# Snake activation by a cosine identity over pairs of PSUM banks, alpha folded into the weights, one stock of banks, a planned order

## The chip, the cores and the metric

The kernel runs on one core of a Trainium2 chip. The time is device microseconds (us) of one launch, as the median of several runs. A core has five engines that run in order, each on its own queue, and meet by semaphores: PE (TensorE), DVE (VectorE), ACT (ScalarE), POOL (GpSimd) and SP, which here only issues DMAs.

## The reference

```python
f = 1 / (1 + exp(-f_logit))                      # q, k, v, f_logit: (4, 8, 768, 48)
for t in range(768):
    state = f[t][:, None] * state + outer(k[t], v[t])
    y[t] = q[t] @ state
x = y, heads side by side                        # (3072, 384)
h = x @ w_in                                     # (3072, 2048)
s = sin(alpha * h)                               # alpha: one number per column of h
out = (h + s * s / (alpha + 1e-9)) @ w_out       # (3072, 384)
```

## The kernel before

The 768 steps are cut into 6 chunks c of 128 steps. A chunk has four batches b, handled in halves: a unit u = 2c + half is two batches. For each unit SP loads f, k, q and v (128x768 float32, 384 KB each, 48 loads in rows of 192 bytes) into three buffers of each kind (`load`).

**Attention.** `pre` (L316 on): ACT turns f into log decay (L327, L330), PE sums it over time with a triangular mask (cs, L350), ACT makes the decay and its inverse (G in place in PSUM, L359; Gi, L363), and two products scale k and q (L372). `attend`: PE transposes them (tp), a copy brings them to SBUF (tr, L416; from chunk 4 on a DMA transpose does both), PE makes scores in two banks (aps, L425), DVE masks each bank by itself (at, L428), PE adds the old state's part and the scores' part (y), and y is copied and transposed into xT (from chunk 3 on by DMA). The state is renewed by kv, sum and st.

**MLP.** `first`: for each of 16 blocks fb of 128 columns, PE makes h (three matmuls of 128x512, one bank; L542), ACT takes the sine with alpha as its scale (L547), somebody squares it (L555 on POOL or DVE, L553 on ACT), and DVE adds (square / alpha) + h into the bfloat16 g (L560). Chunk 0 does this by halves of 256 tokens. `second`: for each batch, 16 matmuls of 128x384 over the blocks g (o, L580), a copy (osb) and a store.

**Banks and order.** PSUM's eight banks are split: 2 for o, 3 for h, 3 for all else. The weights are cast to bfloat16 by DMAs on POOL's queue, held back until certain loads have landed (`weights_after`). The order on each engine comes from a planner, `in_order`, which starts the operation that could begin first by its own table of durations, with tables of biases (KIND, ON_ACT, ...) fitted to it.

Of the kernel before, what the change touches and what calls it, by code (L numbers as in the profile page):

```python
# [71 lines left out]

class Op:
    after, line, on_act = 0, None, 0

    def __init__(self, rank, engs, emit, deps, takes, table, dma):
        self.rank, self.engs, self.emit, self.deps, self.takes = rank, engs, emit, deps, takes
        self.table, self.dma, self.start, self.end, self.eng = table, dma, None, None, None
        self.line = table and "table"


LATENCY = {"PE": 260, "ACT": 160, "DVE": 180, "POOL": 180, "SP": 0}
TABLE_LOAD, DMA_LATENCY, DMA_AHEAD = 1280, 1400, 1000


def in_order(ops, lines):


    free = dict.fromkeys(("PE", "ACT", "DVE", "POOL", "SP"), 2500)
    free["ACT"] = free["SP"] = 800  # L90
    dma_free, table = dict.fromkeys(("SP", "POOL"), 0), None
    follows = {}
    for o in ops:
        for d in set(o.deps):
            follows.setdefault(d, []).append(o)
    missing = {o: len(set(o.deps)) for o in ops}
    done, turn, nth = [], {o: i for x in lines.values() for i, o in enumerate(x)}, dict.fromkeys(lines, 0)

    def when(o):

        t = max([o.after] + [d.end + (LATENCY[d.eng] if d.eng not in o.engs or len(o.engs) > 1 or d.eng != "PE" else 0)
                             for d in o.deps])
        for j, b in enumerate(o.takes):
            if b.place is None:
                i = len(b.ring.taken) + sum(x.ring is b.ring for x in o.takes[:j])
                if i >= b.ring.n:
                    old = b.ring.taken[i - b.ring.n]
                    if any(x.end is None for x in old.users):
                        return None
                    t = max([t] + [x.end + LATENCY[x.eng] for x in old.users])  # L110
        return t

    pending = [o for o in ops if not missing[o]]
    left = len(ops)
    while left:
        best = None
        for o in pending:
            if o.line and turn[o] != nth[o.line]:
                continue
            t = when(o)  # L120
            if t is None:
                continue
            for e, dur in o.engs.items():
                s = max(t, free[e])
                if o.dma:
                    s = max(s, dma_free[e] - DMA_AHEAD)
                d = dur + (TABLE_LOAD if o.table and o.table != table and table else 0)
                key = (s + (BIAS[e] + (o.on_act if e == "ACT" else 0) if len(o.engs) > 1 else 0), o.rank, s + d)
                if best is None or key < best[0]:
                    best = (key, o, e, s, d)  # L130
        if best is None:
            raise RuntimeError("no operation can start")
        _, o, e, s, d = best
        o.start, o.eng, free[e] = s, e, s + d
        o.end = s + d
        if o.dma:
            dma_free[e] = max(s + 600, dma_free[e]) + o.dma
            o.end = dma_free[e] + DMA_LATENCY + (1500 if e == "POOL" else 0)
            if e == "POOL":
                dma_free["SP"] = max(s + 600, dma_free["SP"]) + o.dma  # L140
        table = o.table or table
        if o.line:
            nth[o.line] += 1
        for b in o.takes:
            if b.place is None:
                b.place = len(b.ring.taken)
                b.ring.taken.append(b)
        pending.remove(o)
        for x in follows.get(o, ()):
            missing[x] -= 1  # L150
            if not missing[x]:
                pending.append(x)
        done.append((o, e))
        left -= 1
    return done
# [518 lines left out]
```

## Time and profile before

| | |
|---|---|
| three runs | 217.67, 219.94, 220.72 us, median 219.94 |
| span of the profiled execution | 216.7 us, first to last instruction; that execution's own time is not among the numbers given, and the three runs lie 1.0 to 4.0 us above its span |
| PE, DVE, ACT, POOL busy | 182.6, 157.3, 165.9, 102.4 us |
| mean share of the DMA engines | 72.0% by SP's queue, 9.1% by POOL's |

A busy PE is not a PE at its full rate, since the matmul rows hold their latency too. So the rate is read where matmuls stand back to back, and the work left is counted in matmuls.

### The profile page before, as it was taken

To read this page: it belongs to the slowest core of one execution; us is meant where nothing else is said; L and a number is where in the kernel's file an instruction comes from. 1 tells how busy PE (TensorE), PEld (TensorE's weight loads), DVE (VectorE), ACT (ScalarE), POOL (GpSimd) and SP (SyncE) were. 2 spreads that over 40 slices of the span, in tenths; PEclk is the share of its full clock that TensorE was granted. 3 is DMA by queue.
4 is the path that set the end of the run, shared out by engine and by line. 5 is a ranking of instruction groups with operands and counts; after the bars stand their busy time and mean duration, and the time that the engine had idled before them with its cause. 6 is when DMAs were issued, how large, how long until landed. Compare 5 with 4: busy or idle time off the path is not lost.

```text
span 216.7 us, 4268 instructions
## 1 busy us (share of the span) xinstructions
PE 182.6 (84%) x1537; PEld 107.5 (50%) x1537; DVE 157.3 (73%) x290; ACT 165.9 (77%) x272; POOL 102.4 (47%) x131
## 2 busy tenths in 40 slices
PE   0477785489968999858899987989999999999993
PEld 0345553257655645534565533555554555555551
DVE  2364895475794799897779989579989968787800
ACT  3578778966579979878998999886778888667711
POOL 5334692863543488677575412685324113233100
PEclk9999999658999999979999999999999999999999
DMA  7999999999999999799799993834701211010211
GB/s 130 187 187 217 197 200 187 199 187 199 181 192 190 181 191 168 184 148 155 173 188 182 188 183 93 190 60 146 168 20 39 94 54 41 0 73 2 74 73 73
DMA packets 119733, 30.30 MB, mean 140 GB/s; under 512 B 113040, under 2 KB 119712, under 8 KB 119712
## 3 DMA queue, kind: packets, MB, share of 16 engines
q1 hardware_dynamic: 115968, 26.88, 72.0%
q0 software_dynamic: 3744, 3.15, 9.1%
q8 instruction: 12, 0.20, 0.4%
q14 instruction: 9, 0.07, 0.2%
HBM read 25.17 MB, written 4.72 MB: 138 GB/s over the span
## 4 chain that ended last, share of the span: by engine, by line
PE 59%; DVE 16%; DMA 9%; ACT 5%; issue 5%; SPq 3%; POOL 2%; ACTq 0%; POOLq 0%; DVEq 0%
PE o L580 25%; PE h L542 23%; DMA f<-in_f_logit_dram 6%; DVE g L560 6%; DVE at L428 4%; DMA v<-in_v_dram 3%; SPq L270 3%; PE tp L408 3%; PE aps L425 2%; DVE vb L334 2%; PE y L445 2%; POOL s L555 2%; PE cs L350 1%; DVE sum L481 1%; ACT f L327 1%
## 5 line engine op out<-in xcount | busy, mean ns | idle before, releaser
L555 POOL TENSOR_TENSOR s<-s 128x512 f32<-128x512 f32 (+1 forms) x71 | 61.0, 872 | 64.0 <-ACT s L547 56.5
L547 ACT ACTIVATE s<-h,al_p 128x512 f32<-128x512 f32 (+1 forms) x112 | 67.5, 627 | 22.4 <-PE h L542 18.7
L542 PE MATMUL h<-xT,w_in_bf 128*128 128x512 bf16 (+1 forms) x336 | 78.3, 355 | 6.8 <-DVE g L560 4.8
L580 PE MATMUL o<-w_out_bf,g 128*128 128x384 bf16 x384 | 79.1, 332 | 2.5 <-DVE g L560 2.3
L560 DVE SCALAR_TENSOR_TENSOR g<-s,al_r,h 128x512 bf16<-128x512 f32 (+1 forms) x112 | 72.3, 666 | 10.3 <-POOL s L555 7.4
L580 PEld LDWEIGHTS <-g 128*128 128x128 bf16 x384 | 35.8, 99 | 27.8 <-DVE g L560 3.6
L542 PEld LDWEIGHTS <-w_in_bf 128*128 128x128 bf16 x336 | 32.3, 99 | 31.7 <-issue 8.7
L428 DVE TENSOR_TENSOR at<-aps,mask 128x512 bf16<-128x512 f32 x48 | 31.7, 684 | 4.7 <-PE aps L425 4.5
L372 POOL TENSOR_TENSOR qk<-k,Gi 128x384 bf16<-128x384 f32 x22 | 21.9, 1007 | 24.2 <-ACT Gi L363 24.1
L372 DVE TENSOR_TENSOR qk<-q,cs 128x384 bf16<-128x384 f32 x24 | 13.2, 549 | 11.0 <-ACT cs L359 10.4
L553 ACT ACTIVATE s<-s 128x512 f32<-128x512 f32 x28 | 17.6, 633 | 0.7
L350 PE MATMUL cs<-lf,mask 128*128 128x384 bf16 x24 | 8.2, 358 | 11.0 <-ACT lf L330 9.7
L416 ACT COPY tr<-tp 128x1024 bf16<-128x1024 bf16 x12 | 12.1, 1014 | 3.1 <-PE tp L408 3.0
L642 ACT ACT_TABLE_LOAD x11 | 14.1, 1283 | 0.2
L408 PE MATMUL tp<-ident,qk 128*128 128x128 bf16 x128 | 12.2, 255 | 2.4 <-POOL qk L372 1.9
L363 ACT ACTIVATE Gi<-cs 128x384 f32<-128x384 f32 x24 | 11.6, 485 | 2.6 <-PE cs L353 1.3
L425 PE MATMUL aps<-tr 64*128 64x128 bf16 x192 | 10.9, 231 | 3.1 <-ACT tr L416 2.1
L327 ACT ACTIVATE f<-f 128x768 f32<-128x768 f32 x12 | 10.1, 839 | 4.2 <-DMA f<-in_f_logit_dram 2.8
L485 POOL TENSOR_TENSOR st<-sum,gl 128x384 bf16<-128x384 f32 x12 | 10.2, 860 | 5.7 <-DVE sum L481 5.7
L445 PE MATMUL y<-vb,at 128*128 128x48 bf16 x192 | 11.5, 190 | 1.3 <-DVE at L428 0.7
L408 PEld LDWEIGHTS <-qk 128*128 128x128 bf16 x128 | 10.4, 117 | 4.3 <-POOL qk L372 2.6
L359 ACT ACTIVATE cs<-cs 128x388 f32<-128x388 f32 (+1 forms) x24 | 11.5, 480 | 0.6
(53 smaller groups left out, 150.8 us busy)
## 6 DMA issues: line engine op xcount, KB each, us to landing
f<-in_f_logit_dram SPq DMA_DIRECT2D x12, 384.0 KB, 6.7
k<-in_k_dram SPq DMA_DIRECT2D x12, 384.0 KB, 6.7
q<-in_q_dram SPq DMA_DIRECT2D x12, 384.0 KB, 6.8
v<-in_v_dram SPq DMA_DIRECT2D x12, 384.0 KB, 6.7
out_dram<-osb SPq DMA_DIRECT2D x24, 192.0 KB, 1.9
w_in_bf<-in_moe_w_in_dram POOLq DMA_DIRECT2D x4, 384.0 KB, 8.1
w_out_bf<-in_moe_w_out_dram POOLq DMA_DIRECT2D x4, 384.0 KB, 7.8
xT<-yn SPq DMA_TRANSPOSE x12, 2.3
```

The costliest lines, as they stand in the source:

```text
L372: engine[e].tensor_mul(qk_b[bufs["qk", m].place % NQ][:, "kq".index(n), :, :, :D], tl[n, u][:, i * H:(i + 1) * H, :].rearrange("c (r p) d ...
L408: nc.tensor.transpose(tl[x, "tp"][:, j * HP + p, :], qk_b[qkb.place % NQ][:, j, p, :, :].rearrange("c r e -> c (r e)"), ident)
L425: nc.tensor.matmul(aps[r][:, p, :], t[halves[r], p, :], t[halves[r], HP + p, :], start=True, stop=True)
L428: nc.vector.tensor_mul(tl[x, "at", r], tl[x, "a"][r], mask4)
L445: nc.tensor.matmul(tl[x, "y"][:, h * D:(h + 1) * D], tl[x, "at", r][:, p, :], v_b[vb.place % NV][:, i, h, :], start=(first and p == r == 0 ...
L542: nc.tensor.matmul(h[:, :n], w_in_bf[:, kb, fs], xT[:, ts.start // C:ts.stop // C, kb, :], start=(kb == 0), stop=(kb == KB - 1))
L547: nc.scalar.activation(out=s[:, :n], in_=tl[x, "h"][:, :n], func=Act.Sin, scale=al_p[:, fb:fb + 1])
L553: nc.scalar.activation(out=s2[:, :n], in_=s[:, :n], func=Act.Square)
L555: engine[e].tensor_mul(s2[:, :n], s[:, :n], s[:, :n])
L560: nc.vector.scalar_tensor_tensor(tl["g", c, fb][:, ts], tl[x, "s2"][:, :n], al_r[:, fb:fb + 1], tl[x, "h"][:, :n], Alu.mult, Alu.add)
L580: nc.tensor.matmul(tl["o", c, t], tl["g", c, fb][:, t * P:(t + 1) * P], w_out_bf[:, fb, :], start=(fb == 0), stop=(fb == FB - 1))
L642: nc.scalar.preload_act_table_set(now)
```

## The change

- **Identity.** sin² a = (1 - cos 2a) / 2. `w_in` is multiplied by -2 alpha and `w_out` by -1 / (2 (alpha + 1e-9)). PE then gives h' = -2 alpha h, ACT takes sin(h' + pi/2), and one DVE instruction makes g' = (s - 1) + h'. The 112 squares are gone.
- **Weights.** They come as float32 on SP's queue into three staging buffers `wst` and are folded by eight multiplications (six on POOL, two on DVE). The factor for `w_in` is alpha spread over 128 partitions by four float32 matmuls of one row.
- **Two banks at once.** In chunks 1 to 5 h is made in pairs of blocks in two banks, and sine and addition run once over 128x1024. The masks do the same for the scores. In chunk 0 a pair of half blocks shares one bank.
- **One stock of banks.** All eight banks are one tile, and each buffer's bank comes from the order table.
- **G in SBUF.** The decay leaves PSUM, so POOL can take q's products: it has 17 of them (DVE 7), 18 of k's (DVE 6), and 10 of the 12 casts of v (none before). Of the tr copies DVE makes 14 (4 before), ACT 2 (12 before).
- **Order.** The planner is replaced by a list of 982 numbers (operation, engine, bank), found beforehand.

```diff
+ORDER = [10, 74, 75, 83, 10077, 22, 20008, 85, 2088, 9, 84, 78, 14, 30004, 11, 2005, 137, 138, 40000, 50006,
...
+SLOTS = dict(f=3, k=3, q=3, v=3, lf=2, qk=6, vb=4, gl=6, Gi=4, tr=4, at=3, xT=2, yn=5, s=3, g=18, G=3, osb=3, sum=2,
+             wst=3, st0=2, st1=2, st2=2, st3=2)
...
-    ps_o = pool("ps_o", 2, space=bass.MemoryType.PSUM)
-    ps_h = pool("ps_h", N_H, space=bass.MemoryType.PSUM)
-    ps_a = pool("ps_a", N_A, space=bass.MemoryType.PSUM)
+    banks = psum.tile([P, 8, 512], F32, name="banks")
...
+    nc.vector.memset(ones_f, -2.0)
...
+                nc.tensor.matmul(ps(b, 512), ones_f, al_row[:, fs], start=True, stop=True)
...
+            nc.vector.tensor_scalar(al_r, ps(b, FB), 1e-9, -2.0, Alu.add, Alu.mult)
             nc.vector.reciprocal(al_r, al_r)
...
-                nc.gpsimd.dma_start(out=w_in_bf[:, :, fs], in_=moe_w_in[:, fs].rearrange("(kb p) f -> p kb f", p=P))
...
+        def ld(e):
+            engine[e].dma_start(out=view(), in_=src)
+
+        def fold(e):
+            engine[e].tensor_tensor(dst, view(), fac(), Alu.mult)
+        l = op({SP: 500}, ld, takes=[b], dma=2050)
...
-            g = tl["cs", m][:, :n_G]
-            nc.scalar.activation(out=g, in_=g, func=Act.Exp, scale=-1.0)
...
+                nc.scalar.activation(out=at(Gb)[:, :n_G], in_=ps(cb, n_G), func=Act.Exp, scale=-1.0)
...
-            nc.vector.tensor_mul(tl[x, "at", r], tl[x, "a"][r], mask4)
...
+            nc.vector.tensor_mul(at(atb), ps(ab, 1024).rearrange("c (r p t) -> c r p t", r=2, p=HP),
+                                 mask4.unsqueeze(1).to_broadcast([C, 2, HP, C]))
...
+            nc.scalar.activation(out=at(sb)[:, :n], in_=ps(hb, n), func=Act.Sin, bias=quarter)
...
+            nc.vector.scalar_tensor_tensor(take(at(gb)), at(sb)[:, :n].rearrange("p (j t) -> p j t", j=2), -1.0,
+                                           ps(hb, n).rearrange("p (j t) -> p j t", j=2), Alu.add, Alu.add)
...
-            nc.scalar.activation(out=s[:, :n], in_=tl[x, "h"][:, :n], func=Act.Sin, scale=al_p[:, fb:fb + 1])
...
-                nc.scalar.activation(out=s2[:, :n], in_=s[:, :n], func=Act.Square)
...
-                engine[e].tensor_mul(s2[:, :n], s[:, :n], s[:, :n])
...
-            nc.vector.scalar_tensor_tensor(tl["g", c, fb][:, ts], tl[x, "s2"][:, :n], al_r[:, fb:fb + 1],
-                                           tl[x, "h"][:, :n], Alu.mult, Alu.add)
```

The first place is the weights. Before, POOL issues their DMAs itself, early (`seen` is the wait for a load; the last two rows are a product for k and the first square):

```order
L372 TENSOR_TENSOR qk_87<-k_133,Gi_153 128x8x48
L372 TENSOR_TENSOR qk_88<-k_133,Gi_156 128x8x48
L285 COPY seen<-f_160 1x1
L292 DMA w_in_bf<-in_moe_w_in_dram 128x3x512
L285 COPY seen<-q_183 1x1
L292 DMA w_in_bf<-in_moe_w_in_dram 128x3x512 x3
L372 TENSOR_TENSOR qk_90<-k_218,Gi_299 128x8x48
L555 TENSOR_TENSOR s_0_0_0_370<-s_0_0_314 128x256
```

In the change they stand on SP's queue between the loads. These are its DMAs number 11 to 22, counted from the first load of f:

```order
L219 DMA k_70<-in_k_dram 128x16x48
L219 DMA q_73<-in_q_dram 128x16x48
L219 DMA f_67<-in_f_logit_dram 128x16x48
L274 DMA wst_142<-in_moe_w_in_dram 128x3x512
L274 DMA wst_143<-in_moe_w_in_dram 128x3x512
L274 DMA wst_144<-in_moe_w_in_dram 128x3x512
L219 DMA v_76<-in_v_dram 128x16x48
L274 DMA wst_142<-in_moe_w_in_dram 128x3x512
L274 DMA wst_143<-in_moe_w_out_dram 128x4x384
L274 DMA wst_144<-in_moe_w_out_dram 128x4x384
L219 DMA q_71<-in_q_dram 128x16x48
L219 DMA k_68<-in_k_dram 128x16x48
```

So the first weights moved behind 13 loads, and the first part of `w_out` is DMA number 19; the last part of `w_in` (number 18) and all of `w_out` reuse a staging buffer and wait for its fold.

The second place is DVE in the middle of the program, chunk 2, where blocks of the MLP and masks of the attention alternate. Before:

```order
L555 TENSOR_TENSOR s_1_10_0_1560<-s_10_0_1527 128x512
L560 SCALAR_TENSOR_TENSOR g_10_1578<-s_1_10_0_1560,al_r,h_10_0_1421 128x512
L428 TENSOR_TENSOR at_0_0_1564<-aps_0_0_1566,mask_97 128x512
L428 TENSOR_TENSOR at_0_1_1565<-aps_0_1_1567,mask_97 128x512
L560 SCALAR_TENSOR_TENSOR g_11_1607<-s_1_11_0_1589,al_r,h_11_0_1461 128x512
```

And now, in chunks 2 and 3:

```order
L461 SCALAR_TENSOR_TENSOR g_126<-s_115,banks 128x1024
L409 TENSOR_TENSOR sum_141<-banks,st_145 128x384
L412 TENSOR_TENSOR st_152<-sum_140,gl_91 128x384
L409 TENSOR_TENSOR sum_140<-banks,st_149 128x384
L461 SCALAR_TENSOR_TENSOR g_125<-s_113,banks 128x1024
L371 TENSOR_TENSOR at_104<-banks,mask_159 128x1024
```

The square is gone from the row of instructions, and each addition and mask covers two banks.

On PE, ahead of the first matmul of `second`, stand 63 matmuls of h and 177 of attention before, and 90 of h, 235 of attention and 5 for alpha now. The whole program has 336 of h (96 of 256 tokens, 240 of 512), 384 of o and 816 of attention in both.

## Rows read from the trace of the kernel before

**Rows 1.** The page's part 1: engine, busy us, share, instructions.

```profile
PE 182.6 (84%) x1537; PEld 107.5 (50%) x1537; DVE 157.3 (73%) x290; ACT 165.9 (77%) x272; POOL 102.4 (47%) x131
```

**Rows 2.** Busy time by stage: stretch, length, PE, PEld, DVE, ACT, POOL, granted clock, DMA, GB/s.

```profile
35.00:45.00 10.00, 4.51 (x40) 3.00 (x40) 4.37 (x12) 9.18 (x15) 6.50 (x9) 0.75 1.27 193
60.00:130.00 70.00, 61.44 (x573) 35.92 (x571) 59.22 (x111) 62.00 (x98) 39.98 (x43) 0.98 1.12 178
140.00:200.00 60.00, 59.03 (x431) 31.85 (x430) 49.77 (x76) 46.88 (x77) 23.82 (x24) 1.00 0.26 65
```

**Rows 3.** One line's instructions, L580: ns min/median/max, first and last start us.

```profile
L580 PE MATMUL o<-w_out_bf,g x384: 322/326/528, 44.7 to 212.8; 128*128 128x384 bf16 x192
```

**Rows 4.** PE's groups in the stretch 150 to 217 us: count | busy us, mean ns.

```profile
L580 PE MATMUL o<-w_out_bf,g 128*128 128x384 bf16 x194 | 37.5, 326 | 0.0
L542 PE MATMUL h<-xT,w_in_bf 128*128 128x512 bf16 x128 | 33.0, 379 | 0.0
L445 PE MATMUL y<-vb,at 128*128 128x48 bf16 x48 | 2.7, 184 | 0.0
L437 PE MATMUL y<-st,tr 128*128 128x96 bf16 x24 | 2.0, 206 | 0.0
L425 PE MATMUL aps<-tr 64*128 64x128 bf16 x32 | 1.6, 219 | 0.0
```

**Rows 5.** The chain that ended last: start us, us, what.

```profile
122.57 6.25 DMA v<-in_v_dram
...
203.38 0.65 PE h L542 x3
204.03 9.12 PE o L580 x56
```

**Rows 6.** Groups by line and shape: count | busy us, mean ns | idle before.

```profile
L560 DVE SCALAR_TENSOR_TENSOR g<-s,al_r,h 128x512 bf16<-128x512 f32 x80 | 57.9, 743 | 8.7 <-POOL s L555 6.3 <-ACT s L553 1.5
L547 ACT ACTIVATE s<-h,al_p 128x512 f32<-128x512 f32 x80 | 53.5, 688 | 17.1 <-PE h L542 16.2
L555 POOL TENSOR_TENSOR s<-s 128x512 f32<-128x512 f32 x41 | 42.6, 1048 | 51.0 <-ACT s L547 45.2 <-DVE s L555 3.5 <-DVE g L560 1.9
L428 DVE TENSOR_TENSOR at<-aps,mask 128x512 bf16<-128x512 f32 x48 | 31.7, 684 | 4.7 <-PE aps L425 4.5
L372 POOL TENSOR_TENSOR qk<-k,Gi 128x384 bf16<-128x384 f32 x22 | 21.9, 1007 | 24.2 <-ACT Gi L363 24.1
L555 POOL TENSOR_TENSOR s<-s 128x256 f32<-128x256 f32 x30 | 18.3, 633 | 13.0 <-ACT s L547 11.3 <-DVE g L560 1.4
L553 ACT ACTIVATE s<-s 128x512 f32<-128x512 f32 x28 | 17.6, 633 | 0.7
L560 DVE SCALAR_TENSOR_TENSOR g<-s,al_r,h 128x256 bf16<-128x256 f32 x32 | 14.4, 475 | 1.6 <-POOL s L555 1.1
L547 ACT ACTIVATE s<-h,al_p 128x256 f32<-128x256 f32 x32 | 14.0, 473 | 5.3 <-POOL s L555 2.7 <-PE h L542 2.5
L372 DVE TENSOR_TENSOR qk<-q,cs 128x384 bf16<-128x384 f32 x24 | 13.2, 549 | 11.0 <-ACT cs L359 10.4 <-DMA q<-in_q_dram 0.6
L416 ACT COPY tr<-tp 128x1024 bf16<-128x1024 bf16 x12 | 12.1, 1014 | 3.1 <-PE tp L408 3.0
```

**Rows 7.** Timeline of the start: start us, us, engine, line, what (SPq: a DMA's issue).

```profile
4.87 0.84 ACT L327 ACTIVATE f<-f 128x768 f32<-128x768 f32 x1 [2.78 <-DMA f<-in_f_logit_dram]
6.61 2.03 SPq L270 DMA_DIRECT2D f<-in_f_logit_dram  x1
19.18 1.46 PE L542 MATMUL h<-xT,w_in_bf 128*128 128x256 bf16 x6 [0.94 <-ACT cs L359]
```

**Rows 8.** One line's instructions, the squares on DVE: ns min/median/max.

```profile
L555 DVE TENSOR_TENSOR s<-s x13: 416/692/1473, 33.5 to 202.9; 128x512 f32<-128x512 f32 x11, 128x256 f32<-128x256 f32 x2
```

More of the change, by code (lines that the diff above doesn't have):

```diff
@@ L76, in __init__ @@
[L76 to L92, printed above, removed]
-    for o in ops:
[L94 to L143, printed above, removed]
-        for b in o.takes:
[L145 to L155, printed above, removed]
@@ new lines, in __init__, with in_order @@
+    def __init__(self, engs, emit, deps, takes, table, dma, after):
+        self.engs, self.emit, self.deps, self.takes = engs, emit, deps, takes
+        self.table, self.dma, self.after = table, dma, after
+def in_order(ops):
+    left = {}
+    for o in ops:
+        for b in {b for b in o.uses}:
+            left[b] = left.get(b, 0) + 1
+    held = {n: [(None, -1)] * k for n, k in SLOTS.items()}
+    for nth, x in enumerate(ORDER):
+        o = ops[x % 2000]
+        for b in o.takes:
+            if b.place is None and b.ring == "ps":
+                b.place = x // 10000
+            elif b.place is None:
+                free = [(t, i) for i, (old, t) in enumerate(held[b.ring]) if old is None or not left[old]]
+                b.place = min(free)[1]
+        for b in o.uses:
+            left[b] -= 1
+            if b.ring != "ps":
+                held[b.ring][b.place] = (b, nth)
+        yield o, list(o.engs)[x // 2000 % 5]
@@ L303, in alpha, with mm, ev @@
-    def alpha(rank):
-        b = buf("a")
+    w_in_made, w_out_made, w_ready = {}, {}, {}
+    def alpha():
+        for n in range(4):
+            b = Buf("ps")
+            ab = bufs.setdefault(("al", n // 2), Buf("s"))
+            half = slice(n % 2 * TOK, (n % 2 + 1) * TOK)
+            fs = slice(n * 512, (n + 1) * 512)
+            def mm(e, b=b, fs=fs):
+                nc.tensor.matmul(ps(b, 512), ones_f, al_row[:, fs], start=True, stop=True)
+            def ev(e, b=b, ab=ab, half=half):
+                (nc.scalar.copy if e == ACT else nc.vector.tensor_copy)(at(ab)[:, half], ps(b, 512))
+            m = op({PE: 1700}, mm, takes=[b], after=6000)
+            w_ready["in", n] = op({DVE: 690, ACT: 600}, ev, deps=[m], takes=[ab], holds=[b])
+        b = Buf("ps")
@@ L341, in pre @@
+        x = op({ACT: 840}, exp_, deps=[fb_.ready], holds=[fb_], table=EXP)
+        l = op({ACT: 840}, ln_, deps=[x], takes=[lf], holds=[fb_], table=EXP)
+        made["v", u] = op({DVE: 770, POOL: 840}, values, deps=[vb_.ready], takes=[vv], holds=[vb_])
         for i in range(2):
             m = 2 * u + i
[L343 removed]
+            cb, Gib, Gb, qkb, glb = Buf("ps"), Buf("Gi"), Buf("G"), Buf("qk"), Buf("gl")
             bufs["gl", m], bufs["qk", m] = glb, qkb
@@ L376, in pre @@
-            c_ = op(rank + KIND["cs"][u] + i, {PE: 168 if last else 275}, cs_, deps=[l], takes=[cb], holds=[lf])
-            c_.line = "cs"
-            cs_order.append(c_)
-            gi = op(rank, {ACT: 475}, Gi_, deps=[c_], takes=[Gib], holds=[cb], table=EXP)
-            g = op(rank, {ACT: 475}, G_, deps=[c_], holds=[cb], table=EXP)
-            late += [gi, g]
-            km = lambda e, i=i, m=m: mul(e, i, m, "k", tl["Gi", m])
-            qm = lambda e, i=i, m=m: mul(e, i, m, "q", tl["cs", m])
@@ new lines, in pre @@
+            c_ = op({PE: 166 if last else 265}, cs_, deps=[l], takes=[cb], holds=[lf])
+            gi = op({ACT: 490}, Gi_, deps=[c_], takes=[Gib], holds=[cb], table=EXP)
+            g = op({ACT: 490}, G_, deps=[c_], takes=[Gb], holds=[cb], table=EXP)
+            km = lambda e, i=i, qkb=qkb, Gib=Gib: mul(e, i, qkb, 0, kb_, at(Gib))
+            qm = lambda e, i=i, qkb=qkb, Gb=Gb: mul(e, i, qkb, 1, qb_, at(Gb)[:, :H * D])
+            made["kh", m] = op({POOL: 1010, DVE: 550}, km, deps=[gi, kb_.ready], takes=[qkb], holds=[kb_, Gib])
@@ new lines, in attend, with snake, sin_, add @@
+            bufs["st", c, b] = sb
+    def snake(hb, sb, gb, n, take):
+        def sin_(e):
+            nc.scalar.activation(out=at(sb)[:, :n], in_=ps(hb, n), func=Act.Sin, bias=quarter)
+        def add(e):
+            nc.vector.scalar_tensor_tensor(take(at(gb)), at(sb)[:, :n].rearrange("p (j t) -> p j t", j=2), -1.0,
+                                           ps(hb, n).rearrange("p (j t) -> p j t", j=2), Alu.add, Alu.add)
+        return sin_, add
+    def first(c, fb, needs):
+        hb, sb = Buf("ps", 2), Buf("s")
+        gb = bufs["g", c, fb] = Buf("g")
+        xb = bufs["xT", c]
+        def mm(e, j):
+            f = fb + j
+            for kb in range(KB):
+                nc.tensor.matmul(ps(hb, 2 * TOK)[:, j * TOK:(j + 1) * TOK], w_in_bf[:, kb, f * P:(f + 1) * P],
+                                 at(xb)[:, :, kb, :], start=(kb == 0), stop=(kb == KB - 1))
+        sin_, add = snake(hb, sb, gb, 2 * TOK, lambda t: t)
+        a = None
+        for j in range(2):
+            a = op({PE: 648}, lambda e, j=j: mm(e, j), deps=needs + [a], takes=[hb], holds=[xb])
+        s = op({ACT: 1020}, sin_, deps=[a], takes=[sb], holds=[hb], table=TRIG)
+        made["g", c, fb, 0] = made["g", c, fb, 1] = op({DVE: 1250}, add, deps=[s], takes=[gb], holds=[sb, hb])
@@ new lines, in first_half @@
+    def first_half(c, half, fb, needs):
+        hb, sb = Buf("ps"), Buf("s")
+        gb = bufs.setdefault(("g", c, fb), Buf("g"))
+        xb = bufs["xT", c]
+        ts = slice(2 * half, 2 * half + 2)
+        def mm(e):
+            h = ps(hb, TOK).rearrange("p (j t) -> p j t", j=2)
+            for j in range(2):
+                for kb in range(KB):
+                    nc.tensor.matmul(h[:, j, :], w_in_bf[:, kb, (fb + j) * P:(fb + j + 1) * P], at(xb)[:, ts, kb, :],
+                                     start=(kb == 0), stop=(kb == KB - 1))
+        sin_, add = snake(hb, sb, gb, TOK, lambda t: t[:, :, half * TOK // 2:(half + 1) * TOK // 2])
+        a = op({PE: 660}, mm, deps=needs, takes=[hb], holds=[xb])
+        s = op({ACT: 600}, sin_, deps=[a], takes=[sb], holds=[hb], table=TRIG)
+        made["g", c, fb, half] = op({DVE: 690}, add, deps=[s], takes=[gb], holds=[sb, hb])
@@ L602 @@
+        op({SP: 400}, store, deps=[v_], holds=[sbuf], dma=700)
+    quarter = consts.tile([P, 1], F32)
+    nc.vector.memset(quarter, 1.5707963267948966)
+    alpha()
     for u in range(NCH * NU):
         for n in "fkqv":
-            load(u, n, EARLY)
-    load_order += [bufs[x].ready for x in LOADS]
-    w_in_load(0, EARLY)
-    w_in_load(1, EARLY + 1)
-    w_out_load(EARLY + 2)
-    needs = lambda half, fb: [made["x", 0, 2 * half + i] for i in range(2)] + [w_in_dma[fb // 4]]
-    sins, parts = [], []
+            load(u, n)
@@ L612 @@
+    for n in range(4):
+        weights("in", n)
+    for n in range(4):
+        weights("out", n)
     for u in range(NCH * NU):
         c, half = divmod(u, NU)
-        parts.append(pre(u, RANK[u]))
+        pre(u)
         for b in (2 * half, 2 * half + 1):
-            attend(c, b, base(c) - ATT[c] + 4 * b)
+            attend(c, b)
         if c == 0:
-            for fb in range(FB):
-                sins.append(first(0, fb, HALF[half], 16 * half - 32 + fb, needs(half, fb)))
+            for fb in range(0, FB, 2):
+                first_half(0, half, fb, [made["x", 0, 2 * half + i] for i in range(2)] + [w_in_made[fb // 4]])
@@ L632 @@
-    assert n_sin == len(sins)
+            for fb in range(0, FB, 2):
+                first(c, fb, [made["x", c, b] for b in range(B)] + [w_in_made[fb // 4]])
     for c in range(NCH):
         for t in range(B):
-            second(c, t, base(c) + LAG[c] + 4 * t)
+            second(c, t)
     now = EXP
-    for o, e in in_order(ops, {"table": act_order, "load": load_order, "h": h_order, "cs": cs_order}):
+    for o, e in in_order(ops):
         if o.table and o.table != now:
```

413 lines of the change are left out of this document (148 added, 265 removed), and 75 rows, old and new, of tables (KIND, LOADS, ON_ACT, ORDER).

## The prediction

> **What bounds the kernel now.** I read the stages first, then the chain that ended last, then the groups by shape. The chain ends in 9.12 us of 56 matmuls of o back to back, 0.163 us each; three of h take 0.65, 0.217 each, and I take half of it for 256 columns [rows 5]. At these rates the 194 o and 128 h after 150 us [rows 4] come to 31.6 + 27.8 = 59.4 us. PE ends at 213.2 (204.03 + 9.12), so 63.2 us held them, and 3.8 are left for the 104 attention matmuls (48 y, 24 y, 32 aps): 0.037 each. From 150 us on PE is full, and only less PE work there would help. I take 0.04 for attention, since the earlier stages also hold wider ones.
>
> The first o starts at 44.7 us [rows 3]. By the order PE then still has 384 o (62.6 us), 240 h of 512 (52.1) and 33 of 256 (3.6), and 816 - 177 = 639 of attention (25.6): 143.9 us at rate. It needs 213.2 - 44.7 = 168.5. So **24.6 us are lost between 45 and 150 us**, though PE is busy by the rows: 61.44 of 70 us between 60 and 130 [rows 2]. There ACT is busy 62.0 of 70 us and DVE 59.2, 89% and 85%, at 64% to 98% of a rate that PE could have. Between 140 and 200 us DVE has 83%, ACT 78%, and PE 59.0 of 60: at these shares hardly anything is lost. The reader is to see from the pair that PE loses time where ACT and DVE near nine tenths, in a chain of h, sine, square and addition that holds each bank to its end.
>
> **The change part by part.**
>
> *Squares, sines, additions.* POOL loses 71 squares, 41 x 1.048 + 30 x 0.633 = 62.0 us. ACT loses 28 squares, 17.7, and 80 sines x 0.688 + 32 x 0.473 = 70.2; it gains 16 of 512 columns (11.0) and 40 of 1024 [rows 6]. These are not in the trace: by the step from 256 to 512 columns (0.215 us) they take 0.688 + 0.430 = 1.118, at least 0.86 (the columns alone), at most 1.376 (two of 512). I take 1.118, the same line on: 44.7. ACT falls by 32.2. DVE loses 13 squares at the median 0.692 (9.0) [rows 8] and additions of 80 x 0.743 + 32 x 0.475 = 74.6; it gains 16 x 0.743 and 40 at 0.743 + 2 x 0.268 = 1.279 (1.07 to 1.486), 63.1. Falls by 20.5.
>
> *Masks.* 48 x 0.684 = 32.8 against 24 at about 1.22 (1.07 to 1.368): 3.5 saved on DVE. PE's y now waits for both halves at once, about half a microsecond later for the first; the matmuls of h and o queued around it cover that, and without them it would be 24 x 0.5 = 12 us.
>
> *Moves.* Ten tr copies leave ACT (10.1 us) for DVE (10 x at most 1.014), 17 q products leave DVE (9.3) for POOL (17 x 1.007 = 17.1), and casts too (a cast on POOL between 0.5 and 2 times a product's 1.007; ten are 5 to 20 us, I take 10). POOL has room: 102.4 - 62 leaves 40 us [rows 1], and with casts, products and folds it comes to some 80.
>
> *Weights.* The bytes read from HBM are the same, and moved from POOL's queue to SP's. f lands at 4.9 us and SP issues a load each 2.08 [rows 7]. A fold on POOL by the squares' step (0.415 for 256 columns) is 1.048 + 4 x 0.415 = 2.7 us for 1536 columns (2.5 to 3.1). The first part of w_in, DMA number 14, lands at 4.9 + 13 x 2.08 = 31.9, and h can start at 34.7 instead of 19.2. The last part (18) lands at 40.2, is folded by 42.9, and the first of w_out (19, landed at 42.3) by 45.6. So the **first o comes at about 46 instead of 44.7**. SP waits for staging buffers behind loads of q and k; they are free in time by the same count (number 20 needs the fold of number 16, done at 38.8). PE isn't idle meanwhile: ahead of the first o it now has 90 h and 235 of attention, before 63 and 177. That is 2.9 + 2.3 = 5.2 us of work brought forward.
>
> *Alpha.* Four float32 matmuls, at least 0.22 us each, at most perhaps 2. Four times 2 is 8 us among 35 before h; PE's cover there is that it waits for loads. If it were gone, 8 us. I take nothing.
>
> *Bank stock, table of order.* Eight banks for any use cost no instruction. Two banks of h are held for h, sine, addition, some 1.3 + 1.1 + 1.3 us and the gaps; three pairs in flight leave two banks for o and attention.
>
> **Sum.** DVE has about 157.3 - 20.5 - 3.5 - 9.3 + 10 = 134 us, plus two folds and the like, less casts; ACT 165.9 - 32.2 - 10.1 = 124. After the first o PE has 62.6 + 52.1 + 0.6 + 581 x 0.04 = 138.5 us. Ahead of the first o the order has some 30 us of each, so that 104 and 94 are left beside 138.5 of PE: 75% and 68% of it, under the 83% and 78% at which PE was full [rows 2]. At the loss of that stage (1 in 60) PE would lose 2.3 us. I take 10 of the 24.6: gaps at changes of stage and waits for loads don't go with the squares. What is late next is the loads. The v of chunk 2's second half is SP's number 36, two of the earlier ones small stores: it lands at about 4.9 + 33 x 2.08 + 2 = 75.6, and behind its first use PE has 310 o, 192 h of 512 and some 400 of attention, 50.5 + 41.7 + 16 = 108.2. That bounds the span at 188, ten below the sum.
>
> PE ends at 46 + 138.5 + 10 = 194.5; the last copy and store take 216.7 - 213.2 = 3.5: **span 198.0**. The profiled span lies 3.2 under the median 219.94, so **201 us**. Its own range is 196 (lost 5) to 208 (lost 17).
>
> **The rivals.**
>
> *Loads alone* (better): PE loses nothing else, 188 + 3.2 = 191 us. For it: the shares above; against: no stage before 140 us did so.
>
> *PE loses as much as before*: 46 + 138.5 + 24.6 + 3.5 + 3.2 = 216. The loss then came from latency through the chain, or from loads, rather than from busy engines. For it speaks that DVE and ACT themselves sat idle before additions and sines, 8.7 and 17.1 us [rows 6], and that the DMA engines were full (share 1.12) in the same 60 to 130 us [rows 2].
>
> *SP's queue holds loads back.* Its order now puts 11 loads behind the first DMA transposes, which wait for finished attention; before, the last load was issued at 122.57 [rows 5]. A delay of 8 us in these reaches PE: 209.
>
> *VectorE and GpSimd meet at SBUF.* The squares on DVE (two inputs in SBUF) took 0.692 us at the median, but one took 1.473 beside a busy POOL [rows 8]. With G in SBUF, 13 products, 3 state products and 2 folds have two such inputs on DVE: 18 x 0.78 = 14 us if each waits as long; half on the path gives 208. [...]
>
> [...]
>
> That the change doesn't do what it says isn't a rival: the order shows no square left.
>
> **How the numbers follow.** Forecast (201, range 196 to 208) 0.58; loads alone 0.07; loss as before 0.12; SP's queue 0.09; DVE and POOL 0.07; thin start 0.07. 2% either way, 215.5 and 224.3, is about what can be told from no change. Faster: 0.58 + 0.07 + 0.09 + 0.07, and 0.03 of "loss as before" = 0.84. Same: 0.09 + 0.02 of the thin start = 0.11. Slower: 0.05. The range leaves out most of the better case, the upper half of "loss as before" and the thin start: 193 to 215.
>
> **What would show it.** Right: no squares; sines of about 1.12 us and additions of 1.28; first h near 35 and first o near 46 us; DVE and ACT under 80% between 60 and 130 us; PE at rate from 50 us on, ended near 195; POOL near 80 us. Wrong: first o after 50; granted clock 0.5 before 45 us; products on DVE far over 0.55; ACT or DVE still at 85%; SP's last load issued after 135 us; PE waiting for loads of chunks 3 and 4.

## The result and the profile after

The changed kernel takes **201.82 us** (median; 198.82 to 202.01) against 219.83 for the kernel before on the same chip: ratio 0.9132, 95% interval 0.9031 to 0.9234. The ratio, here and below, leaves out runs more than 1.5% above the fastest of their kernel (here 201.88 and 202.01), so it is not that of the two medians, 0.918. Forecast were 201 us and a range of 193 to 215. The profiled execution took 201.88 us, its span is 200.2. The number came out; of the working behind it three terms did not, and they nearly cancelled.

The page's part 1 of the changed kernel, against [rows 1]:

```profile
PE 180.1 (90%) x1545; PEld 108.9 (54%) x1545; DVE 141.4 (71%) x176; ACT 125.3 (63%) x180; POOL 74.7 (37%) x88
```

Busy time by stage, as in [rows 2]:

```profile
35.00:45.00 10.00, 8.29 (x72) 6.17 (x73) 7.40 (x7) 5.32 (x9) 6.68 (x4) 1.00 0.59 164
45.00:60.00 15.00, 11.84 (x114) 9.30 (x113) 14.76 (x19) 8.99 (x17) 12.61 (x7) 1.00 1.04 263
60.00:130.00 70.00, 70.00 (x699) 42.38 (x698) 59.12 (x75) 56.23 (x79) 28.52 (x37) 1.00 0.89 181
```

PE is busy in all of the 70 us from 60 to 130, where it was busy 61.44 before, and its granted clock stays at 1.00. VectorE is as busy there as before (84% of the stretch), ScalarE is at 80%. Behind 55.3 us the profile shows no wait of PE at all, so with this work for PE what is left to gain lies ahead of that.

The matmuls of o (one line's instructions, as in [rows 3]) and the end of the chain that ended last (as in [rows 5]):

```profile
L505 PE MATMUL banks<-w_out_bf,g x384: 322/326/337, 55.3 to 196.5; 128*128 128x384 bf16 x192
```

```profile
186.73 10.09 PE banks L505 x62
...
196.84 0.48 ACT osb L511
```

The first o starts at 55.3 us instead of 44.7, over nine later than forecast (46). From there PE needs 186.73 + 10.09 - 55.3 = 141.5 us, where 138.5 + 10 were forecast and the kernel before took 168.4.

Groups by shape, as in [rows 6] (L458 the sine, L461 the addition, L371 the mask, L277 the folds, L328 the products, L239 alpha's matmuls):

```profile
L461 DVE SCALAR_TENSOR_TENSOR g<-s,banks 128x1024 bf16<-128x1024 f32 x40 | 48.2, 1218 | 14.6 <-ACT s L458 13.6
L458 ACT ACTIVATE s<-banks,quarter 128x1024 f32<-128x1024 f32 x40 | 44.3, 1115 | 19.8 <-PE banks L473 19.5
L371 DVE TENSOR_TENSOR at<-banks,mask 128x1024 bf16<-128x1024 f32 x24 | 29.2, 1221 | 6.7 <-PE banks L367 4.5 <-issue 2.0
L277 POOL TENSOR_TENSOR w_in_bf<-wst,s 128x1536 bf16<-128x1536 f32 x3 | 10.3, 3419 | 2.1 <-DMA wst<-in_moe_w_in_dram 2.1
L277 POOL TENSOR_TENSOR w_out_bf<-wst,al_r 128x1536 bf16<-128x1536 f32 x3 | 8.5, 2849 | 1.8 <-DMA wst<-in_moe_w_out_dram 1.8
L328 DVE TENSOR_TENSOR qk<-q,G 128x384 bf16<-128x384 f32 x7 | 7.1, 1008 | 0.8 <-ACT G L318 0.8
L239 PE MATMUL banks<-al_row,ones_f 1*128 1x512 f32 x8 | 7.5, 1093 | 0.0
```

The wide sine and mask cost what the line through the narrow ones said, the addition 5% less. The folds of w_in don't (3.42 us, not 2.7; those of w_out take 2.75, one of them 3.06 beside VectorE), and the q G product on VectorE has a mean of 1008 ns, where it was 549.

Timeline of the start, first VectorE's four slow instructions with its own fold and a mask for comparison, then GpSimd (start us, us):

```profile
29.88 3.48 DVE L328 TENSOR_TENSOR qk<-q,G 128x384 bf16<-128x384 f32 x1
...
37.52 1.75 DVE L277 TENSOR_TENSOR w_in_bf<-wst,s 128x1536 bf16<-128x1536 f32 x1
39.19 1.22 DVE L371 TENSOR_TENSOR at<-banks,mask 128x1024 bf16<-128x1024 f32 x1
...
43.30 3.38 DVE L296 CAST vb<-v 128x768 bf16<-128x768 f32 x1
...
49.75 2.26 DVE L324 TENSOR_TENSOR gl<-G,bd 128x8 f32<-128x8 f32 x1
...
57.88 1.91 DVE L328 TENSOR_TENSOR qk<-k,Gi 128x384 bf16<-128x384 f32 x1
```

```profile
29.52 3.42 POOL L277 TENSOR_TENSOR w_in_bf<-wst,s 128x1536 bf16<-128x1536 f32 x1 [2.14 <-DMA wst<-in_moe_w_in_dram]
38.31 1.01 POOL L324 TENSOR_TENSOR gl<-G,bd 128x8 f32<-128x8 f32 x1 [5.37 <-ACT G L318]
39.29 3.42 POOL L277 TENSOR_TENSOR w_in_bf<-wst,s 128x1536 bf16<-128x1536 f32 x1
...
42.84 3.42 POOL L277 TENSOR_TENSOR w_in_bf<-wst,s 128x1536 bf16<-128x1536 f32 x1
46.22 5.76 POOL L277 TENSOR_TENSOR w_out_bf<-wst,al_r 128x1536 bf16<-128x1536 f32 x2
...
56.64 2.75 POOL L277 TENSOR_TENSOR w_out_bf<-wst,al_r 128x1536 bf16<-128x1536 f32 x1 [1.77 <-DMA wst<-in_moe_w_out_dram]
```

Read ends, not starts: the product ends at 33.36, the fold beside it at 32.94; the cast at 46.68, its fold at 46.26; gl at 52.01, the pair of folds at 51.98; the k Gi product at 59.79, its fold at 59.39. Each starts inside a GpSimd fold and ends with it. Undisturbed they take 0.55, 0.55, 0.16 and 0.55 us, so 9.2 us are waits. Masks and additions, which have one of their inputs in PSUM, ran beside folds at their usual length in this trace (the mask at 39.19 beside the fold from 39.29 on: 1.22 us; two additions from 46.60 beside the folds from 46.22 on: 1.27, as the two from 61.39 with no fold). It goes the other way as well: GpSimd's gl, 0.20 us elsewhere, took 1.01 at 38.31 while VectorE folded.

Three of the four, all but the k Gi product, lie ahead of the first o and on the chain that ended last, and so do alpha's matmuls:

```profile
7.55 5.31 PE banks L239 x6
...
14.66 2.00 PE banks L239 x2
...
29.96 3.41 DVE qk L328
...
43.38 3.31 DVE vb L296
...
49.83 2.18 DVE gl L324
```

### The profile page after: what moved, and what is told of

It reads as the page before. It is cut to its first block, busy times and chain, and to the rows that moved or that the text cites. A ratio compares the mean times of both kernels' runs of the same rounds, so it can differ in the third digit from the quotient of the medians.

```text
span 200.2 us, 3887 instructions
## 1 busy us (share of the span) xinstructions
PE 180.1 (90%) x1545; PEld 108.9 (54%) x1545; DVE 141.4 (71%) x176; ACT 125.3 (63%) x180; POOL 74.7 (37%) x88
## 4 chain that ended last, share of the span: by engine, by line
PE 85%; DVE 9%; ACT 2%; DMA 2%; issue 1%; DVEq 0%
PE banks L505 32%; PE banks L473 26%; PE banks L360 5%; PE banks L367 4%; PE banks L239 4%; PE banks L492 3%; PE banks L310 3%; PE banks L383 2%; DVE qk L328 2%; DMA f<-in_f_logit_dram 2%; PE banks L377 2%; PE banks L401 2%; DVE vb L296 2%; DVE g L461 1%; PE banks L391 1%; DVE gl L324 1%
## 5 line engine op out<-in xcount | busy, mean ns | idle before, releaser
L505 PE MATMUL banks<-w_out_bf,g 128*128 128x384 bf16 x384 | 73.3, 326 | 0.0
L458 ACT ACTIVATE s<-banks,quarter 128x1024 f32<-128x1024 f32 (+1 forms) x56 | 54.4, 993 | 27.1 <-PE banks L473 19.5
L461 DVE SCALAR_TENSOR_TENSOR g<-s,banks 128x1024 bf16<-128x1024 f32 (+1 forms) x56 | 58.3, 1064 | 16.9 <-ACT s L458 15.9
L473 PE MATMUL banks<-xT,w_in_bf 128*128 128x512 bf16 x240 | 55.1, 379 | 0.0
L371 DVE TENSOR_TENSOR at<-banks,mask 128x1024 bf16<-128x1024 f32 x24 | 29.2, 1221 | 6.7 <-PE banks L367 4.5
L328 POOL TENSOR_TENSOR qk<-k,Gi 128x384 bf16<-128x384 f32 x18 | 18.2, 1018 | 11.2 <-PE banks L313 2.8
L328 POOL TENSOR_TENSOR qk<-q,G 128x384 bf16<-128x384 f32 x17 | 17.3, 1021 | 13.1 <-DMA q<-in_q_dram 7.5
L318 ACT ACTIVATE G<-banks 128x388 f32<-128x388 f32 (+1 forms) x24 | 11.7, 493 | 7.3 <-DVE qk L328 3.1
L360 PE MATMUL banks<-ident,qk 128*128 128x128 bf16 x128 | 13.2, 253 | 2.6 <-DVE qk L328 2.6
L492 PE MATMUL banks<-xT,w_in_bf 128*128 128x256 bf16 x96 | 13.1, 294 | 1.4 <-DVE g L461 1.4
L321 ACT ACTIVATE Gi<-banks 128x384 f32<-128x384 f32 x24 | 11.6, 492 | 4.4 <-PE banks L313 4.3
```

Source lines behind the costliest of these rows:

```text
L328: engine[e].tensor_mul(at(qkb)[:, j, :, :, :D], at(src)[:, i * H:(i + 1) * H, :].rearrange("c (r p) d -> c p r d", r=2), g.rearrange("c (p ...
L360: nc.tensor.transpose(ps(tpb, 1024, BF16)[:, (j * HP + p) * C:(j * HP + p + 1) * C], at(qkb)[:, j, p, :, :].rearrange("c r e -> c (r e)"), ...
L371: nc.vector.tensor_mul(at(atb), ps(ab, 1024).rearrange("c (r p t) -> c r p t", r=2, p=HP), mask4.unsqueeze(1).to_broadcast([C, 2, HP, C]))
L458: nc.scalar.activation(out=at(sb)[:, :n], in_=ps(hb, n), func=Act.Sin, bias=quarter)
L461: nc.vector.scalar_tensor_tensor(take(at(gb)), at(sb)[:, :n].rearrange("p (j t) -> p j t", j=2), -1.0, ps(hb, n).rearrange("p (j t) -> p j ...
L473: nc.tensor.matmul(ps(hb, 2 * TOK)[:, j * TOK:(j + 1) * TOK], w_in_bf[:, kb, f * P:(f + 1) * P], at(xb)[:, :, kb, :], start=(kb == 0), sto ...
```

## The experiments

Three questions: is it the squares' work that held PE (theory A), what made the start late (theory C), and can both be had? All twelve in one table. PE's time is from the start of the first o to the end of the last; ratios are to the kernel before on the same chip, with their 95% intervals. The last two columns are those of the profiled execution. It took as long as the median or within 1.5 us of it, but for e1 (241.75 us, 4.0 over), e10 (197.74, 2.5 over), e5 (201.21, 1.8 over) and e2 (198.98, 3.0 under). The edits are shortened.

| kernel | time, us | ratio | first o, us | PE from there, us |
|---|---|---|---|---|
| before | 219.8 | 1 | 44.7 | 168.4 |
| changed | 201.82 | 0.913 (0.903 to 0.923) | 55.3 | 141.5 |
| e1 squares back | 237.75 | 1.083 (1.077 to 1.089) | 62.3 | 174.4 |
| e2 512-wide | 201.96 | 0.912 (0.902 to 0.921) | 52.3 | 141.5 |
| e3 identity alone | 234.31 | 1.062 (1.054 to 1.071) | 43.7 | 186.5 |
| e4 folds in pieces | 196.55 | 0.894 (0.889 to 0.898) | 50.2 | 141.5 |
| e5 alpha by DMA | 199.37 | 0.905 (0.898 to 0.913) | 50.1 | 146.1 |
| e6 four buffers | 194.87 | 0.887 (0.881 to 0.892) | 48.2 | 141.5 |
| e7 old order | 216.17 | 0.985 (0.976 to 0.993) | 44.1 | 167.1 |
| e8 stop, no work | 208.86 | 0.952 (0.944 to 0.959) | 57.6 | 146.1 |
| e9 alpha in four rows | 195.26 | 0.890 (0.886 to 0.893) | 48.4 | 141.5 |
| e10 fourth alpha matmul earlier | 195.26 | 0.886 (0.881 to 0.891) | 49.1 | 143.6 |
| e11 folds on VectorE | 202.27 | 0.921 (0.917 to 0.926) | 55.4 | 141.5 |
| e12 w_out's folds on ScalarE | 199.00 | 0.906 (0.902 to 0.910) | 50.9 | 143.0 |

**e1, the identity undone in the new order.**

```
-  Sin(h', bias=quarter)
+  s = Sin(h', scale=-0.5); then s = s * s on "PAPPDPAP"[nth % 8] (POOL, ACT, DVE)
-  g = (s - 1) + h'
+  g = -2 s + h'
```

> The changed kernel with the identity alone undone: sine of alpha h (scale -0.5 of the folded h), a square in place behind it (GpSimd 25 + 10, ScalarE 10 + 4, VectorE 5 + 2 of the 40 wide and 16 narrow ones), then h' - 2 s2. Folds, bank stock, two-bank width and order stay. Theory A (the squares' work and their place in the chain of h, sine, square, addition cost PE its time in the middle): GpSimd gains 25 x 1.88 + 10 x 1.05 = 57 us, the chain of each pair of banks grows by 1 to 2 us, PE loses 10 to 25 us more behind the first o: 211 to 226 us. Rival B (order and bank stock did it, squares find idle engines): 201 to 206 us.

237.75 us, worse than any theory gave and worse than before. What waited between 55 and 230 us (engine, line, releaser: us, times, longest; L467 the square, L461 the sine, L470 the addition, L482 h):

```profile
POOL s L467 <- ACT s L461: 47.4, 15, 11.9
DVE g L470 <- POOL s L467: 36.6, 24, 5.4
ACT s L461 <- PE banks L482: 29.2, 20, 4.0
PE banks L482 <- DVE g L470: 14.8, 12, 2.4
```

Every engine waits for the next one round the ring, though none is full:

```profile
60.00:130.00 70.00, 61.79 (x613) 37.75 (x612) 53.58 (x69) 49.20 (x73) 49.98 (x47) 0.98 0.76 149
```

VectorE is at 77%, ScalarE at 70%, GpSimd at 71%, and PE loses 8 us of 70, as much as the kernel before with VectorE at 85% and ScalarE at 89% [rows 2].

**e8, the stops of e1 without its work.** Same engines, same places, eight columns:

```
+  s[:, 0:8] = s[:, 0:8] * 1.0 on "PAPPDPAP"[nth % 8], behind each sine
```

> The changed kernel with a multiplication by 1 of eight columns of each sine, on the engine and at the place in its queue where e1 has the square: the same stops of the chain at GpSimd (35), ScalarE (14) and VectorE (7), nearly no work. Theory A1 (in e1 the squares' own duration, 1.75 us on GpSimd, cost the 36 us): 202 to 208. Rival (the stop itself, a third engine's queue between sine and addition, costs most of it): 218 to 236.

208.86 us: just above A1's 202 to 208. The stop at a third queue costs 7.0 us, 2.3 of them ahead of the first o; the other 28.9 us of e1's 35.9 go with the squares' duration (35 on GpSimd, mean 1753 ns) in a chain whose order was made without them.

**e3 and e7, the identity in the old kernel.** e3 lets the planner plan anew; e7 plans with squares and issues none.

```
-  s = Sin(h, scale=al_p); s2 = s * s; g = s2 * al_r + h        # al_p = alpha, al_r = 1 / alpha
+  s = Sin(h, scale=al_p, bias=quarter); g = s * al_r + h       # al_p = 2 alpha, al_r = -1 / (2 alpha)
```

> The kernel before with the identity alone: sine of 2 alpha h + pi/2 on ScalarE, then h - sine / (2 alpha) on VectorE, no squares; the constant 1/(2 alpha) is left out. Weights, alpha's place, bank pools, 512-wide pieces and the old planner's rules stay (it plans anew without squares). Theory A (relief): GpSimd -62 us, ScalarE -18, VectorE -9, and most of the 24.6 us that PE lost between 45 and 150 us go: 203 to 210. Rival B (the old order, its thin stretch at 35 to 45 us and the low clock there made the loss): 214 to 220.

> The kernel before with the identity, the constant 1/(2 alpha) left out, as in e3, but in the old kernel's own order: the planner still plans with squares and none is issued, so that every other instruction keeps its engine and its place in its queue. Theory A (squares' work and their place in the chain cost PE 24.6 us, whatever the order): 203 to 211 us. Rival B (the old order, its thin stretch at 35 to 50 us and the low clock there hold PE): 214 to 220. e3, which let the planner plan anew, took 234, so that its rules without squares gave a worse order.

Both leave out the constant 1 / (2 alpha) of the identity; e7 also has six buffers for sines. e3 took 234.31: rival B and beyond. e7 took 216.17: rival B. With 61 us less on GpSimd the old order gives back 3.5 of the 18 us (219.7 on the same chip). One blemish: with two per-partition operands the sine is longer than the 688 ns of [rows 6]:

```profile
L549 ACT ACTIVATE s<-h,quarter,al_p 128x512 f32<-128x512 f32 x80 | 60.3, 778 | 26.9 <-PE h L544 26.4
```

So ScalarE is busy 157.6 us, 8 less than before instead of 18 less; GpSimd (41.1) and VectorE (146.1) are freed in full. In e7's stretch from 60 to 130 us it is still busy 60.10 of 70, 86%. How much of the old order's loss is ScalarE's stays open. The granted clock is no better either, 0.67 in 35 to 45 us in both.

**e2, one-bank instructions.**

```
-  Sin, addition on [:, :1024]
+  for x in (0, 512): Sin, addition on [:, x:x + 512]
```

> The changed kernel with each 1024-wide sine and addition as two of 512, one bank each; all else stays. ScalarE gains 40 x (2 x 0.689 - 1.115) = 10.5 us, VectorE 40 x (2 x 0.677 - 1.218) = 5.4 us. Theory A (PE has slack engines now, at 56 and 59 of 70 us): within 2 us of the changed kernel, 200 to 204. Rival (the fixed cost per instruction is what kept VectorE and ScalarE at nine tenths): the loss in the middle comes back, 208 to 215.

201.96 us, theory A's number, for another reason than A's. The stretch from 95 to 130 us, of the kernel before and of e2:

```profile
95.00:130.00 35.00, 32.23 (x264) 18.01 (x262) 29.61 (x53) 30.80 (x50) 19.09 (x21) 0.96 1.17 179
```

```profile
95.00:130.00 35.00, 35.00 (x311) 19.48 (x309) 29.76 (x47) 30.48 (x51) 14.72 (x20) 1.00 0.83 171
```

VectorE is at 85% in both, ScalarE at 88% and 87%; PE loses 2.8 us in the one and nothing in the other. The share of busy time alone does not decide.

In e2's profiled execution the q G product began at 29.76 us, ahead of the fold (29.94), and took 0.54 us; in the changed kernel's it began 0.36 behind the fold and took 3.48. The spans differ by 3.0 us (197.2 and 200.2). One of the changed kernel's four runs took 198.82 and three 201.77 to 202.01, a like step; that the same race made it is not shown, since that run has no trace here.

**e4, GpSimd's folds in pieces.**

```
-  engine[e].tensor_tensor(dst, view(), fac(), Alu.mult)
+  for i in range(dst.shape[1]): nc.gpsimd.tensor_tensor(dst[:, i], view()[:, i], fac()[:, i], Alu.mult)
```

> The changed kernel with each GpSimd fold of 1536 columns cut into three (w_in) or four (w_out) instructions; the same work. In the trace of the changed kernel VectorE's q G product, cast of v, bd product and k Gi product took 3.48, 3.38, 2.26 and 1.91 us and each ended 0.0 to 0.4 us behind the end of a GpSimd fold. Theory C (VectorE is shut out until the running GpSimd instruction ends, and this delays the start): none of the four is over 1.7 us, the first o comes 2 to 5 us before 55.3, time 197 to 200. Rival (VectorE gets in only when GpSimd's queue is empty, or the start waits for loads anyway): the long ones stay or the first o stays at 55, 201 to 203.

196.55 us, half a us under theory C's 197 to 200, with a ratio below the changed kernel's interval. The four instructions:

```profile
29.95 1.47 DVE L332 TENSOR_TENSOR qk<-q,G 128x384 bf16<-128x384 f32 x1
...
41.35 1.51 DVE L300 CAST vb<-v 128x768 bf16<-128x768 f32 x1
...
46.29 0.54 DVE L328 TENSOR_TENSOR gl<-G,bd 128x8 f32<-128x8 f32 x1
...
52.83 1.01 DVE L332 TENSOR_TENSOR qk<-k,Gi 128x384 bf16<-128x384 f32 x1
```

Their waits fall from 9.2 to 2.7 us, those of the three ahead of the first o from 7.9 to 2.3; the first o comes 5.1 us earlier and the time falls by 5.3, though GpSimd's folds got longer in sum (22.8 us, from 18.8). Theory C's mechanism holds: each ends 0.0 to 0.4 us behind the end of the GpSimd instruction that it started in, while the next one of GpSimd's queue already runs. So in e4 VectorE was let in at the end of the running instruction, not of the queue. It cost GpSimd something in turn: one piece of w_out, beside VectorE's own fold, took 2.34 us, where the median one takes 0.83.

**e5, alpha by one broadcasting DMA** (on e4).

```
-  4 x matmul(ones_f, al_row[:, fs]), 4 copies from PSUM
+  dma_start(al_all, alpha broadcast to 128 partitions); 4 x al_all[:, fs] *= -2
```

> e4_fold_pieces with alpha spread over the partitions by one broadcasting DMA on ScalarE's queue (1 MB written) and doubled in place there, instead of by four float32 matmuls; these also no longer hold two of the three sine buffers. In the trace the eight passes take PE 7.3 us between 7.6 and 16.7 us, and the chain that ended last runs through them. Theory C (the start is a chain through PE, and each us off it brings the first o forward): first o 2 to 5 us before 50.2, time 192 to 195. Rival 1 (PE then waits for loads and VectorE instead): 196 to 197. Rival 2 (the broadcast takes the DMA engines some 3 us and pushes every load back): 198 to 200.

199.37 us, rival 2. SP's fourth load is issued at 7.27 us instead of e4's 4.62, and those behind it up to 30 us are 2.6 to 3.7 us late, the last part of w_in 4.0 (37.84, not 33.80). The first o still comes at 50.1, so taking alpha off PE seems to have made up for this at the start; but then PE waits for a product on GpSimd:

```profile
PE banks L363 <- POOL qk L331: 2.7, 1, 2.7
```

GpSimd does not wait for k or q there. The product stands in GpSimd's queue behind folds that began 2.7 us later than in e4 (43.85 us, not 41.18), after a wait of 1.69 for that part of w_in; and it took 2.51 us instead of 1.00, beside VectorE's own fold of w_out. That is one execution, 1.8 us over the median.

**e6 and e9, alpha's rows in four partitions, with and without a fourth staging buffer** (on e4).

```
-  al_row = [1, 2048];  matmul(ps, ones_f, al_row[:, fs])
+  al_row = [97, 512], row n in partition 32 n;  matmul(ps, ones_f[32n:32n+1], al_row[32n:32n+1])
-  wst=3
+  wst=4        # e6 only
```

> e4_fold_pieces with four staging buffers for weights instead of three (alpha's row lies in four partitions to make room). In the trace of e4 SP issues nothing between 27.1 and 33.8 us and the fourth part of w_in then waits for the first fold, the first part of w_out (37.4) for the second. Theory C (staging holds the start): fourth part issued near 27, first o 1 to 4 us before 50.2, time 193 to 196. Rival (GpSimd's folds follow each other at their own pace, so the loads' waits cost nothing): 196 to 197.

> e6 changed two things: in its trace the six passes of alpha's first three matmuls, whose rows now lie in different partitions, ran beside each other and took PE 2.18 us instead of 5.46, and there is a fourth staging buffer. Here e4 with alpha's rows in four partitions alone, three staging buffers. Theory (PE's time in alpha's matmuls is on the chain, staging is not): as e6, 194 to 195.5. Rival (the fourth buffer gave e6 its 1.7 us): as e4, 196 to 197.

194.87 and 195.26 us, with intervals that overlap: e6 fell in theory C's range, but e9 comes to the same without the fourth buffer, so staging costs nothing that can be measured, although SP waits for it, and what both share against e4 is alpha's rows. Against e4 the first o comes 1.8 us earlier in e9 and 2.0 in e6. The three first matmuls of alpha, changed kernel and e6:

```profile
7.40 5.46 PE L239 MATMUL banks<-al_row,ones_f 1*128 1x512 f32 x6
```

```profile
7.27 2.18 PE L240 MATMUL banks<-al_row,ones_f 1*128 1x512 f32 x6
```

Part of the 1.8 us may be the race again: in both, the q G product came ahead of the fold (29.1 us) and took 0.55.

**e10, the fourth alpha matmul beside the others** (on e6; one number of the order moved).

> e6 with the fourth of alpha's matmuls (2.07 us of PE at 13.7 us) moved up in the order beside the other three. Theory (each us of alpha's matmuls on PE delays the start): 1 to 2 us less than e6, 193 to 194. Rival (at 14 us PE waits for loads of k and q anyway): as e6, 194.5 to 195.5.

195.26 us (193.78 to 197.74): the rival. The profiled execution lost 1.9 us of PE on a fold of w_out; the medians show no gain, and the spread would hide one of 1 us.

**e11 and e12, folds off GpSimd** (on e9).

```
-  GpSimd: 3 (w_in) or 4 (w_out) pieces
+  e11: nc.vector.tensor_tensor(dst, view(), fac(), Alu.mult)            # all folds
+  e12: 4 x nc.scalar.mul(dst[:, i], view()[:, i], al_r column)          # w_out alone
```

> e9 with every fold whole on VectorE, at the same places of the order; GpSimd folds nothing. A fold on VectorE took 1.75 us against some 4 in pieces on GpSimd, and no VectorE instruction waits for a GpSimd fold any more, but VectorE gets 6 x 1.75 = 10.5 us more between 29 and 60 us, where it is busy 29 of 35 us. Theory (VectorE has as much to gain from the waits that go as it takes on): 194 to 197. Rival (VectorE becomes the bound there and delays masks and additions): 198 to 202.

> e9 with w_out's three GpSimd folds on ScalarE instead, four copies of 384 columns each with alpha's factor as their scale (12 x 0.48 = 5.8 us of ScalarE, which is busy 11 to 12 of 15 us between 45 and 60); GpSimd loses some 11 us there, and VectorE's waits for it. Theory (ScalarE has the room): 193 to 195. Rival (the copies stand before sines in ScalarE's queue and hold h's banks): 196 to 199.

202.27 and 199.00 us: the rivals, both (e11 0.3 us above its range). The stretch from 45 to 60 us of e11 and of e12:

```profile
45.00:60.00 15.00, 10.67 (x75) 7.47 (x74) 13.79 (x17) 7.00 (x13) 2.94 (x3) 0.89 1.07 266
```

```profile
45.00:60.00 15.00, 12.21 (x101) 8.46 (x98) 10.14 (x15) 12.85 (x24) 2.96 (x3) 1.00 0.97 233
```

In e11 PE waits 4.2 us in one piece for an addition behind VectorE's folds; in e12 ScalarE's copies (606 ns each) stand ahead of sines and tr copies, and the first o is 2.5 us later than in e9. Of the three places tried, GpSimd in pieces (e9) is the best: the engine that the chain waits for least, in instructions short enough for the one that they shut out.

## Why the prediction was right, and where not

- **Sizes of the wide operations**: right. Sine 1.115 us (1.118 forecast), mask 1.221 (1.22), addition 1.218 (1.279; in its bounds). ScalarE has 125.3 us (124), GpSimd 74.7 (80). VectorE has 141.4, not 134; the 9.2 us of waits account for the difference and more.
- **The start**: mis-sized by 9.3 us (first o at 55.3, not 46). The loads were not late: the first part of w_in was there at 29.5, 2.4 us before the count. What was wrong: a fold of w_in on GpSimd takes 3.42 us (2.7 from the squares' step, which fits w_out's 2.75; four k Gi products of 384 columns, 1.007 each in [rows 6], would have given 4.0 for 1536); the folds shut VectorE out (5.1 us by e4); alpha's matmuls, of which the prediction says "I take nothing", are on the chain that ended last with 7.3 us, of which e9 took back up to 1.8. The 2.4 us between e9's 48.4 and 46 are not assigned.
- **Staging buffers, "free in time"**: they were not (SP issued no load between 33.8 and 39.3 us), but e6 against e9 shows that it cost nothing.
- **The loss behind the first o**: forecast 10 of the old 24.6; there were 3.0 against the 138.5 at rate, and as five other kernels, whose first o comes at 48.2 to 55.4 us, need the same 141.5 us and the changed kernel's profile has no wait of PE there, these 3.0 are the rate that I took (2% too good), not a loss. So the start's +9.3 and the middle's -7 cancelled to a PE that ends at 196.8 instead of 194.5.
- **From span to time**: forecast 3.2 us, measured 1.7 (201.88 and 200.2). The 3.2 compared the median with the span of another execution; in each run on record the time lies 1.6 to 1.8 us above that run's own span. This took 1.5 us off again, and 201 met 201.82.
- **The reason given for that loss**, that PE loses time where ScalarE and VectorE near nine tenths: this step failed. The prediction wanted both under 80% between 60 and 130 us; in the changed kernel they have 84% (VectorE) and 80%, and PE loses nothing. e2 runs PE at rate beside 85% and 87%; e1 loses 8 of 70 us with no engine above 77%. e7 says less: it takes the squares' work out of the old order and gains 3.5 us, but leaves ScalarE at 86%. In the place of the shares the runs put the chain: the same prediction's "chain of h, sine, square and addition" costs 36 us when squares are put back into the new order, 29 of them with their duration (e1, e8), while the identity put into the old planner costs 14 (e3). I read this as an order that is good for the chain of durations it was made for, and the gain as one of the identity and its order together; no run isolates that. An order made for the squares in the same way as this one was not tried. Nor was it tried which of the new table, the single stock of banks, G in SBUF, the moved products and alpha's fold makes up the 14.4 us between e7 and the changed kernel; that stays open.
- **Signs of being wrong.** Three that the prediction named came true though the time was met: the first o after 50, products on VectorE far over 0.55 us, SP's last load issued after 135 us (136.6); VectorE's 84% comes close to a fourth.
- **Rivals.** *Loads alone* (191): PE lost nothing behind the first o, but no load bounded it; without the late start the time would be about 192.5 (201.8 - 9.3, an estimate), and e6 has 194.9. *PE loses as before*: no, but e7 still loses 23.2 us (167.1 against 143.9 at rate), so the latency named there was a fair worry. *SP's queue*: its last load came 14 us later than before (122.6), and PE waited for none. *VectorE and GpSimd meet*: it happened, in the start, and harder than priced: four waits of 1.4 to 2.9 us instead of eighteen of 0.78; 5 us by e4. Each of the four started inside a fold and ended 0.03 to 0.42 us behind the fold's end, a cast (3.38 us) among them; I had taken the one slow square of [rows 8] for the price instead of the length of the instruction in the way. *Thin start* (chance 0.07), a PE slowed by a low granted clock ahead of the first o: no run shows it making the changed kernel slower. In the kernel before, the clock was 0.50 between 40 and 50 us, and three matmuls of o took 1.16 us there (at 44.70), 0.65 at 50.62. In the changed kernel it was 1.00 in every stretch up to 130 us, also from 30 to 35, where PE was busy 2.25 of 5; and e2, with 0.75 between 35 and 45 us, had its first o 2.9 us earlier than the changed kernel:

```profile
35.00:45.00 10.00, 8.53 (x75) 6.57 (x76) 7.65 (x6) 4.96 (x8) 9.61 (x5) 0.75 0.93 268
```
